# Attention and a gated MLP on one core: 29 of 36 weight tiles prepared beside the MLP's products, a second score tile turned by DMA, rows to combine loaded earlier

## The chip, the cores and the metric

The kernel runs on one core of a Trainium2 chip. The core has five engines that work side by side, each through its own queue of instructions in order: PE (TensorE, matrix products; PEld is its loading of weights), DVE (VectorE), ACT (ScalarE), POOL (GpSimd) and SP (SyncE, which here issues the DMAs). They meet through semaphores alone. The metric is the time of one execution in microseconds (us). Before the change it is 2955.62 us, the median of three runs (2955.44 to 2955.67).

## What is computed

The reference is one transformer block of 2048 rows and width 576: a normalisation modulated by a condition c, attention with 32 query heads over the last 512 keys of 16 cached heads, a residual, a second modulated normalisation, a gated MLP of width 4608, and a residual.

```python
mod = (silu(c) @ w_mod).reshape(1, 6, 1, -1)      # sa, ca, ga, sb, cb, gb
h = layernorm(x) * (1 + ca) + sa
q = (h @ wq) per head                             # 32 heads of 128
p = softmax(q @ k.T * 128 ** -0.5)                # 512 keys, head h uses cache head h // 2
x = x + ga * ((p @ v) @ wo)
h = layernorm(x) * (1 + cb) + sb
x = x + gb * ((silu(h @ w1) * (h @ w3)) @ w2)
```

All of it is done to about fp32's precision: each operand of a product is split into a high part (fp32r, as PE rounds it) and a low part, the rest, and three products stand for one.

## The kernel before

**Attention.** The 2048 rows are four blocks of 512. A *slot* is one head with one block, 128 of them (`slots`, numbers 0 to 127); slots 0 to 63 hold blocks 0 and 1, the others blocks 2 and 3. A slot has four *steps*, one for each tile of 128 rows. In a step PE makes the scores of a tile (L466 to L468), DVE their maximum (L470) and ACT the exponential (L479, `weights`). The tile p must then be turned, keys to the partitions, as two fp16 parts. That is done in one of two ways. By PE (`turn_by_pe`): three steps after the exponential four transposes against the identity (L505) put it into a PSUM bank of `t_bank` (two of them), ACT makes the high part (L509) and DVE the low one (L515). By DMA (`halve`, then `turned_by_dma`, L351): the exponential itself goes to a bank of `t_bank`, ACT and DVE make the two parts from there, and a transposing DMA, issued two steps after the low part, turns both. `BY_DMA` names the tiles of a slot that go by DMA: tile 0. At the end of the next slot PE multiplies with the values (L530, `values`) and over the following steps with the output weights into the bank pe (L428), which DVE adds into the rows `acc` (L547). Between these stand the query projections (`quad`, matrix qy and qx at L797): a product of two row blocks by two halves of weights is done with seven products instead of eight (Strassen's scheme, names p1 to p7), and so needs seven prepared combinations of the rows (`hdram`) and seven of each weight tile (`wdram`).

**Preparation beside attention.** ACT and POOL prepare these combinations ahead, in DRAM. `set_piece` does a weight tile: load 768 KB raw, four sums on POOL, for each of seven combinations a rounding on ACT (L692), two low parts on POOL (L697, L698), and a store. `rows_pieces` does the same for w2, `h_item` for the rows. `lay` spreads these items over the steps from number 13 on and again from 272 on: it gives each piece a POOL cost, keeps a pace (`PACE`), issues an item's loads (`fill`) `LEAD` = 3 steps before its first piece, and emits a piece's sums, high part, low part and store in four successive steps (`work`). There are 36 gate and up tiles (f = 0 to 35) and 19 pieces of w2, and the rows of three of four families.

**The MLP.** `mlp` runs 72 *groups* (m0 to m71): 36 tiles f with rows 0 to 1023 and then the same tiles with rows 1024 to 2047. A group is seven products p1, p2, p6, p7, p5, p3, p4 (L797, sums in the banks py and px) with one or two *down* products after most of them (`down`, L910), which alternate between the banks pe and pf. DVE adds each into `acc` or `sums` (L904), and only then can PE use that bank again. A group gives the gated activations of 128 columns for two row blocks; an even group and the odd one behind it make the pair that the down products of the next two groups use. After p2 DVE adds (L991), after p5 adds (L999), after p3 multiplies (L1003), after p4 adds and multiplies (L1005, L1006). `act_steps` makes the high and low parts of the activations: ACT L109, the low ones L110 on POOL (one of seven on DVE), and sums on POOL (L943, L950, L958, L959). The prepared set of the next group is loaded tile by tile (`load_wset`, L789) into a pool of eight buffers, tag w. During groups 12 to 30 POOL and ACT also combine rows 1024 to 2047 (`combine`, `stage`, L605 to L635). At groups 37 and 38 `finish` and `finish_rows` add up the first 1024 rows, on POOL and DVE. `split_x` subtracts one half of a block's columns from the other on POOL (L1220), for the second pair of blocks in group 14.

`acc`, the raw weights and the rows to combine share four wide buffers (tag x); in the MLP all four hold `acc`.

`at(slot or group, step, task)` puts a task behind a step; `run` emits what stands there. The order on each engine is the order in which the program emits it.

Of the kernel before, what the change touches and what calls it, by code (L numbers as in the profile page):

```python
# [8 lines left out]
F32 = mybir.dt.float32  # L9
F32R = mybir.dt.float32r  # L10
# [7 lines left out]
P = 128  # L18
# [16 lines left out]
EARLY, LATE = 13, 68  # L35
A1_AT, M0_AT = 24, 70
M0_ITEM = 16
ROOM, LEAD = 600, 3
WLEAD = 4
PACE = 3300, 3100  # L40
MORE, A1_ITEM = 0, 3

ORDERED = {mybir.EngineType.PE, mybir.EngineType.DVE, mybir.EngineType.Activation, mybir.EngineType.Pool, mybir.EngineType.SP}
SCALE = float(DH) ** -0.5
LIFT = 2.0**14
BY_DMA = (0,)
AFTER_EXP = 3
SETTLE = 2
TINY = 1e-30
# [3 lines left out]
def tile_block(  # L53
# [39 lines left out]
    def t_bank():  # L93
        return tpool.tile([P, 512], F32, tag="T", name="pt")
# [378 lines left out]
    def weights(i, t, pss, nm):  # L473
        st = state[i]
        turn(4 * i + t)
        if t == 0:
            st["l"] = odd.tile([P, ST], F32, tag="l", name="l", bufs=4)
        p = t_bank() if t in BY_DMA else pool.tile([P, SB], F32, tag="p", name="p", bufs=PB)
        nc.scalar.activation(p, pss, AF.Exp, bias=nm, accum_out=st["l"][:, t : t + 1])  # L479
        st["p", t] = p  # L480

    due, ways = {}, {}

    def into(st):
        if "pt" not in st:
# [3 lines left out]
    def halve(g):  # L489

        i, t = divmod(g - 1, 4)
        if 0 <= g - 1 < 4 * n and t in BY_DMA:
            st = state[i]
            p12 = pool.tile([P, 2, SB], F16, tag="p", name="p12", bufs=PB)
            nc.scalar.activation(p12[:, 0, :], st["p", t], AF.Copy, scale=LIFT)
            due.setdefault(g, []).append((st.pop(("p", t)), p12[:, 0, :], p12[:, 1, :], (t, p12)))

    def turn_by_pe(g):

        i, t = divmod(g - AFTER_EXP, 4)  # L500
        if 0 <= i < n and t not in BY_DMA:
            st = state[i]
            p, ps = st.pop(("p", t)), t_bank()
            for j in range(KC):
                nc.tensor.transpose(ps[:, j * P : (j + 1) * P], p[:, j * P : (j + 1) * P], ident)  # L505
            cols = slice(t * P, (t + 1) * P)
            ps = ps.rearrange("p (j n) -> p j n", j=KC)
            hi, lo = (into(st)[:, e, :, cols] for e in range(2))
            nc.scalar.activation(hi, ps, AF.Copy, scale=LIFT)  # L509
            due.setdefault(g, []).append((ps, hi, lo, None))  # L510
# [162 lines left out]
    def set_piece(f, n):  # L673

        def views():
            return [works[f][:, k] for k in range(6)]

        k, which = (("p2", 1), ("p1", 0), ("p4", 3), ("p5", 4), ("p6", 5), ("p7", 2), ("p3", 1))[n]

        def prep():  # L680
            a11, a12, a21, a22, s1, s2 = views()
            if n == 0:
                nc.gpsimd.tensor_add(s1, a21, a22)
                nc.gpsimd.tensor_sub(s2, s1, a11)
            elif n == 1:
                nc.gpsimd.tensor_sub(a21, a11, a21)
            elif n == 6:
                nc.gpsimd.tensor_sub(a12, a12, s2)

        def high():  # L690
            x, t = views()[which], staging([P, DC + 1, P], "wmade")
            nc.scalar.copy(t[:, :3, :], x)  # L692
            return x, t

        def low(xt):
            x, t = xt
            nc.gpsimd.tensor_sub(t[:, 3:, :], x[:, :2, :], t[:, :2, :].bitcast(F32))  # L697
            nc.gpsimd.tensor_sub(t[DR:, 2, :], x[DR:, 2, :], t[DR:, 2, :].bitcast(F32))  # L698
            if n == 6:
                del works[f]  # L700

        def put_out(xt):
            nc.sync.dma_start(wdram[f, k][:, :, :], xt[1].bitcast(F32))

        return (0 if n == 6 else None, (2040, 1020, 0, 0, 0, 0, 1020)[n], 1200), (prep, high, low, put_out)

    DOWN = (("p4", "p7"), ("p6",), ("p1", "p5"), ("p2", "p3"))
    G = NF // 2
# [449 lines left out]

    mlp_items = []
    for p in range(G + 1):  # L1160
        mlp_items += [w_item(f) for f in (2 * p, 2 * p + 1) if p < G]
        mlp_items.append(r_item(p))

    def lay(items, first, STEP):

        spare = []

        def cost(task, args):
            if task is put:
                return {split_in: 1580, split_out: 1440}.get(args[2], 0)  # L1170
            return {gate: 1440, last_q: 1300, lower_v: 1300, norm_rows: 330, make_h: 1300}.get(task, 0)

        def pass_fixed(upto):
            while clock[0] < upto:
                fixed = sum(cost(*job) for job in tasks.get(divmod(clock[0], 4), ()))
                clock[1] = max(clock[1], clock[0] * STEP) + fixed
                clock[0] += 1

        clock = [first - 4, 0]
        step, ends = first, []  # L1180
        for number, (fill, pieces) in enumerate(items):
            begin = ends[number - 2] + 1 if number > 1 else first - LEAD + number
            at(*divmod(begin, 4), fill)
            step, when = max(step, begin + LEAD), []
            for (behind, ahead, after), jobs in pieces:
                if behind is not None:
                    step = max(step, when[behind] + 2)
                pass_fixed(step + 1)
                while clock[1] + ahead + after > (step + 1) * STEP + ROOM:
                    step += 1  # L1190
                    pass_fixed(step + 1)
                clock[1] += ahead + after
                when.append(step)
                work(step, *jobs)
            ends.append(step + 2)
        return step
# [14 lines left out]
    for g in range(last_group):  # L1211
        for k, name in enumerate(ORDER):
            if groups[g][1] == groups[g + 1][1]:
                at(("m", g), k, keep_wset, g, name)
            else:
                at(("m", g), k, load_wset, g + 1, name)
    def split_x(pair):

        a = acc[2 * pair + 1]
        nc.gpsimd.tensor_sub(a[:, :, :HALF], a[:, :, :HALF], a[:, :, HALF:])  # L1220

    for d in range(2 * G):
# [6 lines left out]
            times = ((4, (g, 2)), (3, (g, 4)))  # L1229
        for q, (i, t) in times:  # L1230
            at(("m", i), t, load_oset, d, q)
    for pair, i in ((0, ("m", 0)), (1, ("m", 14))):
        at(i, 0, split_x, pair)
    at(("m", 2), -1, begin_sums, 0)
    at(("m", 2 * G + 2), 3, begin_sums, 1)

# [60 lines left out]
    for b in (2, 3):  # L1297
        for t in range(ST):
            at(("m", b), t, norm_stats, b, t)
        at(("m", 4), 1, norm_root, b)  # L1300
    for b, g in ((2, 6), (3, 9)):
        at(("m", g), 0, norm_scale, b)
        for t in range(ST):
            at(("m", g), t, norm_rows, b, t)
        for m in range(DC + 1):
            at(("m", g + 1 + m // 3), 2 * (m % 3), store_h, "M1", b, m, "AS"[m % 2], "raw")
    at(("m", 12), -1, begin_parts, "M1")
    for c in range(3):
        g = 12 + 6 * c
# [247 lines left out]
```

## Time and profile before

| | |
|---|---|
| median of three runs | 2955.62 us |
| the profiled execution | 2954.41 us |
| its span, first to last instruction | 2952.6 us |
| mean granted clock of PE | 0.998 |
| slots 64 to 119 | about 896 to 1628 us |
| the MLP's first 36 groups | about 1712 to 2340 us |

The page and the answers of the trace give times from the span's start. A row of instructions reads: line, engine, operation, what it writes and from what it reads, shape, count, then busy time in us and the mean of one in ns, and what ended the idle time before them. In the order of time a row is: start, length, engine, line, operation, and in brackets the idle time before it with its releaser. Matmuls are pipelined, so the time that one costs is read from the start of the next.

### The profile page before, as it was taken

What the parts mean: (1) busy time and instruction counts of PE and PEld (TensorE: products, weight loads), DVE (VectorE), ACT (ScalarE), POOL (GpSimd) and SP (SyncE); (2) the same over time, 40 slices, a digit from 0 to 9 for tenths busy, and PEclk for the clock granted to TensorE, in tenths of its full rate; (3) what the DMA queues carried; (4) which work ended last, traced back from release to release, by engine and by line L of the source; (5) the groups of instructions that cost most, each with busy time, mean ns of one, the idle gap of its engine ahead of it and who ended that gap; (6) DMA issues with size and microseconds to landing.
All of it is one profiled execution on the core that took longest, in us unless ns stands there. A gap on an engine that the chain in (4) does not pass through costs nothing.

```text
span 2952.6 us, 47355 instructions
## 1 busy us (share of the span) xinstructions
PE 2903.8 (98%) x16056; PEld 2384.8 (81%) x16056; DVE 2011.1 (68%) x3149; ACT 1560.9 (53%) x3251; POOL 1751.2 (59%) x1884
## 2 busy tenths in 40 slices
PE   7999999999999999999999999999999999999999
PEld 6777777777777777777777778888888888888887
DVE  7877787777777877777777766555555555555556
ACT  6667777777656776677677543333333222222322
POOL 3678888888712877777878223355564544334345
PEclk9999999999999999999999999999999999999999
DMA  6989999999885999989889946677766766666664
GB/s 216 280 266 347 277 345 311 298 289 299 260 277 179 326 301 295 296 284 283 273 278 299 300 154 202 218 233 251 251 226 202 286 231 199 205 198 193 202 201 143
DMA packets 441205, 751.27 MB, mean 254 GB/s; under 512 B 185730, under 2 KB 185730, under 8 KB 437380
## 3 DMA queue, kind: packets, MB, share of 16 engines
q1 hardware_dynamic: 440964, 748.25, 79.1%
q8 instruction: 128, 2.10, 0.3%
q14 instruction: 113, 0.93, 0.1%
HBM read 474.97 MB, written 235.37 MB: 241 GB/s over the span
## 4 chain that ended last, share of the span: by engine, by line
PE 80%; DVE 7%; ACT 4%; issue 2%; POOL 1%; DMA 1%; SPq 0%; ACTq 0%; POOLq 0%; DVEq 0%
PE py L797 15%; PE px L797 11%; PE po L530 10%; PE pe L428 10%; PE pf L910 7%; PE pe L910 7%; PE qy L797 5%; PE pt L505 4%; PE qx L797 3%; PE pss L466 2%; PE pss L468 2%; PE pss L467 2%; DVE nm L470 1%; DVE pt L515 1%; DVE acc L547 1%
## 5 line engine op out<-in xcount | busy, mean ns | idle before, releaser
L797 PE MATMUL py<-hset,wset 128*128 128x512 f32 x2016 | 507.2, 391 | 0.0
L547 DVE SCALAR_TENSOR_TENSOR acc<-pe,r,acc 128x576 f32<-128x576 f32 x510 | 413.6, 811 | 58.1 <-PE pe L428 55.4
L797 PEld LDWEIGHTS py<-hset,wset 128*128 128x128 f32 x2016 | 362.4, 188 | 59.0 <-ACT u L998 0.2
L428 PEld LDWEIGHTS pe<-o,oth 128*128 128x128 f32 x2040 | 319.7, 188 | 79.4 <-DVE acc L547 41.6
L797 PE MATMUL px<-hset,wset 128*128 128x512 f32 x1512 | 380.5, 391 | 0.0
L428 PE MATMUL pe<-o,oth 128*128 128x288 f32 x2040 | 360.1, 298 | 12.9 <-DVE acc L547 11.8
L530 PE MATMUL po<-pt,v 128*128 128x512 f16 x1536 | 353.8, 380 | 0.3 <-DMA v<-vs 0.3
L470 DVE TENSOR_REDUCE nm<-pss 128x1 f32<-128x512 f32 x512 | 345.6, 675 | 7.3 <-PE pss L468 7.1
L479 ACT ACTIVATE p<-pss,nm 128x512 f32<-128x512 f32 x384 | 265.7, 692 | 144.7 <-DVE nm L470 141.5
L697 POOL TENSOR_TENSOR wmade<-wraw,wmade 128x256 fp32r<-128x256 f32 x364 | 272.8, 749 | 115.5 <-issue 49.5
L110 POOL TENSOR_TENSOR akv<-u,akv 128x512 fp32r<-128x512 f32 x141 | 182.7, 1307 | 228.8 <-ACT akv L109 227.9
L797 PEld LDWEIGHTS px<-hset,wset 128*128 128x128 f32 x1512 | 275.5, 188 | 49.4
L509 ACT ACTIVATE pt<-pt 128x512 f16<-128x512 f32 x384 | 229.7, 598 | 136.6 <-PE pt L505 134.9
L535 DVE SCALAR_TENSOR_TENSOR otl<-po,undo,oth 128x512 fp32r<-128x512 f32 x128 | 96.1, 751 | 278.7 <-ACT oth L534 272.9
L515 DVE SCALAR_TENSOR_TENSOR pt<-pt 128x512 f16<-128x512 f32 x384 | 261.7, 681 | 28.7 <-ACT pt L509 28.3
L530 PEld LDWEIGHTS <-v 128*128 128x128 f16 x1536 | 140.6, 98 | 160.3 <-DMA v<-vs 0.6
L505 PEld LDWEIGHTS pt<-ident,p 128*128 128x128 f32 x1536 | 186.0, 140 | 72.0 <-PE pss L468 15.7
L505 PE MATMUL pt<-ident,p 128*128 128x128 f32 x1536 | 231.2, 273 | 9.4 <-DVE pt L515 6.4
L797 PE MATMUL qy<-hset,wset 128*128 128x512 f32 x784 | 237.0, 413 | 0.0
L466 PE MATMUL pss<-kh,qh 128*128 128x512 f32 x512 | 227.2, 444 | 6.3 <-ACT qh L109 2.2
L428 PE MATMUL pe<-o,otl 128*128 128x288 f32 x1020 | 217.5, 294 | 0.0
L468 PE MATMUL pss<-kh,ql 128*128 128x512 f32 x512 | 201.3, 393 | 0.9 <-DVE ql L110 0.9
(250 smaller groups left out, 5974.9 us busy)
## 6 DMA issues: line engine op xcount, KB each, us to landing
oset<-od SPq DMA_DIRECT2D x106, 576.0 KB, 4.7
od<-omade SPq DMA_DIRECT2D x133, 288.0 KB, 4.1
wraw<-in_B_w SPq DMA_DIRECT2D x36, 768.0 KB, 6.4
kept<-o SPq DMA_DIRECT2D x64, 288.0 KB, 5.1
o<-kept SPq DMA_DIRECT2D x32, 576.0 KB, 5.8
wraw<-in_A_wq_pairs SPq DMA_DIRECT2D x16, 768.0 KB, 6.3
w2raw<-in_B_w SPq DMA_DIRECT2D x38, 288.0 KB, 4.3
oset<-od SPq DMA_DIRECT2D x35, 288.0 KB, 3.2
```

The costliest lines, as they stand in the source:

```text
L428: nc.tensor.matmul(ps[:, h, :HALF], a[:, rows], b[:, h * HALF : (h + 1) * HALF], start=n == 0, stop=n == 2)
L466: nc.tensor.matmul(pss, st["qh"][:, rows], kh, start=True, stop=False)
L468: nc.tensor.matmul(pss, st["ql"][:, rows], kh, start=False, stop=True)
L470: nc.vector.tensor_reduce(nm, pss, axis=AX.X, op=ALU.max, negate=True)
L479: nc.scalar.activation(p, pss, AF.Exp, bias=nm, accum_out=st["l"][:, t : t + 1])
L505: nc.tensor.transpose(ps[:, j * P : (j + 1) * P], p[:, j * P : (j + 1) * P], ident)
L515: nc.vector.scalar_tensor_tensor(lo, p, LIFT, hi, op0=ALU.mult, op1=ALU.subtract)
L530: nc.tensor.matmul(po, v[:, d, j, :], pt[:, e, j, :], start=k == 0, stop=k == 3 * KC - 1)
L547: nc.vector.scalar_tensor_tensor(a, ps[:, :, :HALF], st["r"][:, t : t + 1], a, op0=ALU.mult, op1=ALU.add)
L697: nc.gpsimd.tensor_sub(t[:, 3:, :], x[:, :2, :], t[:, :2, :].bitcast(F32))
L797: nc.tensor.matmul(ps, w[:, a, :], h[:, b, :], start=start and n == 0, stop=n == 6, skip_group_check=True)
L910: nc.tensor.matmul(ps[:, h, :HALF], a[:, rows], w[:, b, :], start=m == 0, stop=m == 2)
```

## The change

- **Weight tiles.** `mlp_items` keeps only tiles f < `MADE_LATE` = 7. Tiles 7 to 35 are prepared in the group before the one that uses them: `load_raw` two groups ahead, then for each of the seven combinations `make_high` (the sums on POOL, the rounding on ACT, straight into the buffer that PE reads) behind the step at which `load_wset` stood, `make_low` (the two low parts, on DVE) one step later, and, for the tiles that the second pass loads, `keep_set` (the store) four steps later. The items that remain in `lay` move up: the last ends at step 351 (slot 87), before at step 486.
- **Spills.** Blocks 2 and 3 of `acc` are spilled in group 4 and loaded again in groups 34 and 35; the rows for their normalisation are loaded apart (`fetch_rows`), and `split_x` of the second pair moves from group 14 to group 37, behind step 5.
- **Tiles by DMA.** `BY_DMA` has three sets of tiles with the slots at which they begin and end: tile 0, and tiles 0 and 2 in slots 64 to 119 (65 to 120 counted from one).
- **Rows to combine.** Where an item is one of rows, its first piece comes `FAR` = 3 steps later behind its loads.

PE in slot 96, steps 0 to 1, from the scores (pss) through the transposes (pt), the projection (qy) and the output product (pe); before:

```order
L505 MATMUL pt<-ident,p 128x128 x4
L797 MATMUL qy<-hset,wset 128x512 x3
L428 MATMUL pe<-o,oth 128x288 x4
L428 MATMUL pe<-o,otl 128x288 x2
L466 MATMUL pss<-kh,qh 128x512
L467 MATMUL pss<-kl,qh 128x512
L468 MATMUL pss<-kh,ql 128x512
L505 MATMUL pt<-ident,p 128x128 x4
L797 MATMUL qy<-hset,wset 128x512 x4
```

The same place after (lines have moved):

```order
L510 MATMUL pt<-ident,p 128x128 x4
L828 MATMUL qy<-hset,wset 128x512 x3
L429 MATMUL pe<-o,oth 128x288 x4
L429 MATMUL pe<-o,otl 128x288 x2
L467 MATMUL pss<-kh,qh 128x512
L468 MATMUL pss<-kl,qh 128x512
L469 MATMUL pss<-kh,ql 128x512
L828 MATMUL qy<-hset,wset 128x512 x4
```

The four transposes of step 1 are gone; they turned tile 2 of the slot before.

DVE where group 33 passes to group 34, from p3's multiplication to the first down products of group 34 (u, s: activations; aal: a low part; acc: output rows); before:

```order
L1003 TENSOR_TENSOR u_27093<-u_27093,s_27123 128x512
L110 TENSOR_TENSOR aal<-u_27093,aah 128x512
L1005 TENSOR_TENSOR u_27052<-px,u_27052 128x512
L1006 TENSOR_TENSOR u_27052<-u_27052,s_27011 128x512
L904 TENSOR_TENSOR acc_21163<-pe,acc_21163 128x576
L904 TENSOR_TENSOR acc_21168<-pf,acc_21168 128x576
```

After, with the low parts of set 34 (wset from wraw, for p5, p3 and p4):

```order
L1034 TENSOR_TENSOR u_26494<-u_26494,s_26529 128x512
L111 TENSOR_TENSOR aal<-u_26494,aah 128x512
L730 TENSOR_TENSOR wset<-wraw,wset 128x256
L731 TENSOR_TENSOR wset<-wraw,wset 64x128
L1036 TENSOR_TENSOR u_26447<-px,u_26447 128x512
L1037 TENSOR_TENSOR u_26447<-u_26447,s_26399 128x512
L935 TENSOR_TENSOR acc_19806<-pe,acc_19806 128x576
L730 TENSOR_TENSOR wset<-wraw,wset 128x256
L731 TENSOR_TENSOR wset<-wraw,wset 64x128
L730 TENSOR_TENSOR wset<-wraw,wset 128x256
L731 TENSOR_TENSOR wset<-wraw,wset 64x128
L935 TENSOR_TENSOR acc_19811<-pf,acc_19811 128x576
```

One pair of low parts now stands between DVE's L110 and the addition that frees the bank pe, two more pairs before the one that frees pf.

POOL at the same place, sums and low parts of activations (u, aal, akv); before:

```order
L958 TENSOR_TENSOR u_26948<-u_26948,u_27093 128x512
L959 TENSOR_TENSOR u_26904<-u_26948,u_26904 128x512
L110 TENSOR_TENSOR aal<-u_26904,aah 128x512
L110 TENSOR_TENSOR akv<-u_26948,akv 128x512
```

After, with three of the four sums of set 35 (wraw; s1, s2 and the difference for p2):

```order
L989 TENSOR_TENSOR u_26322<-u_26322,u_26494 128x512
L990 TENSOR_TENSOR u_26272<-u_26322,u_26272 128x512
L716 TENSOR_TENSOR wraw<-wraw 128x384
L717 TENSOR_TENSOR wraw<-wraw 128x384
L111 TENSOR_TENSOR aal<-u_26272,aah 128x512
L719 TENSOR_TENSOR wraw<-wraw 128x384
L111 TENSOR_TENSOR akv<-u_26322,akv 128x512
```

The sums s1 and s2 follow the activations' sums directly.

The diff, cut to its core:

```diff
-ROOM, LEAD = 600, 3
+ROOM, LEAD, FAR = 600, 3, 3
+MADE_LATE = 7
-BY_DMA = (0,)
+BY_DMA = ((0,), (0, 2), (0, 2)), (64, 80, 120)
...
-        p = t_bank() if t in BY_DMA else pool.tile([P, SB], F32, tag="p", name="p", bufs=PB)
+        p = t_bank() if t in by_dma(i) else pool.tile([P, SB], F32, tag="p", name="p", bufs=PB)
...
+    def by_dma(i):
+        (few, more, most), (a, b, c) = BY_DMA
+        return few if i < a or i >= c else more if i < b else most
...
+    def make_high(f, k):
+
+        a11, a12, a21, a22, s1, s2 = [works[f][:, j] for j in range(6)]
+        if k == "p1":
+            nc.gpsimd.tensor_add(s1, a21, a22)
+            nc.gpsimd.tensor_sub(s2, s1, a11)
+        elif k == "p2":
+            nc.gpsimd.tensor_sub(a21, a11, a21)
+        elif k == "p7":
+            nc.gpsimd.tensor_sub(a12, a12, s2)
+        x = {"p1": a11, "p2": a12, "p6": s2, "p7": a21, "p5": s1, "p3": a12, "p4": a22}[k]
+        t = sets[f, k] = pool.tile([P, DC + 1, P], F32R, tag="w", name="wset", bufs=8)
+        nc.scalar.copy(t[:, :3, :], x)
+        works[f, k] = x, t
+
+    def make_low(f, k):
+
+        x, t = works[f, k]
+        nc.vector.tensor_sub(t[:, 3:, :], x[:, :2, :], t[:, :2, :].bitcast(F32))
+        nc.vector.tensor_sub(t[DR:, 2, :], x[DR:, 2, :], t[DR:, 2, :].bitcast(F32))
+        if k == ORDER[-1]:
+            del works[f]
+
+    def keep_set(f, k):
+        nc.sync.dma_start(wdram[f, k][:, :, :], works.pop((f, k))[1].bitcast(F32))
...
-        mlp_items += [w_item(f) for f in (2 * p, 2 * p + 1) if p < G]
+        mlp_items += [w_item(f) for f in (2 * p, 2 * p + 1) if f < MADE_LATE]
...
-            step, when = max(step, begin + LEAD), []
+            step, when = max(step, begin + LEAD + FAR * (fill.__name__ == "fill")), []
...
+            elif MADE_LATE <= g + 1 < NF:
+                for late, task in enumerate((make_high, make_low, keep_set)[: 2 + (g + 2 < NF)]):
+                    m, step = divmod(8 * g + k + 1 + late * late, 8)
+                    at(("m", m), step - 1, task, g + 1, name)
             else:
                 at(("m", g), k, load_wset, g + 1, name)
+    for f in range(MADE_LATE, NF):
+        at(("m", f - 2), 4, load_raw, f)
...
-    for pair, i in ((0, ("m", 0)), (1, ("m", 14))):
-        at(i, 0, split_x, pair)
+    for pair, i in ((0, ("m", 0)), (1, ("m", NF + 1))):
+        at(i, 5 * pair, split_x, pair)
...
+        at(("m", 4), 2, spill, b)
+        at(("m", NF + b - 2), (4, 0)[b - 2], load_x, b)
     for b, g in ((2, 6), (3, 9)):
+        at(("m", g - 1), 4, fetch_rows, b)
...
+        at(("m", g + 2), 3, rows.pop, b)
```

More of the change, by code (lines that the diff above doesn't have):

```diff
@@ L491, in halve @@
         i, t = divmod(g - 1, 4)
-        if 0 <= g - 1 < 4 * n and t in BY_DMA:
+        if 0 <= g - 1 < 4 * n and t in by_dma(i):
             st = state[i]
@@ L500, in turn_by_pe @@
         i, t = divmod(g - AFTER_EXP, 4)
-        if 0 <= i < n and t not in BY_DMA:
+        if 0 <= i < n and t not in by_dma(i):
             st = state[i]
```

## The prediction

> **What bounds the kernel now.** I read the page's busy shares first, then the busy time by stage, then who waited for whom on PE, and last the order of time at the places that the change touches.
>
> ```profile
> PE 2903.8 (98%) x16056; PEld 2384.8 (81%) x16056; DVE 2011.1 (68%) x3149; ACT 1560.9 (53%) x3251; POOL 1751.2 (59%) x1884
> ...
> 900.00:1628.00 728.00, 720.38 (x4065) 563.30 (x4065) 558.49 (x903) 510.21 (x1146) 542.77 (x695) 1.00 0.90 284
> 1712.00:2340.00 628.00, 627.04 (x3424) 550.70 (x3423) 356.77 (x506) 207.53 (x359) 294.67 (x228) 1.00 0.68 227
> ```
>
> The columns of the stages are length, then busy time of PE, PEld, DVE, ACT and POOL, granted clock, DMA share and GB/s. The first stage holds slots 64 to 119, where tiles are to be turned by DMA; the second is the gate and up products of the first 1024 rows, where the weights are now to be prepared. PE is busy for 720 of 728 and 627 of 628 us at full clock. So only two things can shorten this kernel, less work on PE or the few waits of PE in the attention slots; and any new wait of PE is lost in full. In the product stage DVE is busy for 57%, ACT for 33%, POOL for 47%.
>
> Who waited on PE between 896 and 1628 us (total, times, longest):
>
> ```profile
> PE pt L505 <- DVE pt L515: 2.7, 13, 0.3
> PE pe L428 <- DVE acc L547: 2.1, 4, 0.7
> PE pt L505 <- DVE p L515: 1.8, 1, 1.8
> ...
> PEld pe L428 <- DVE acc L547: 13.7, 31, 1.1
> ...
> PEld pt L505 <- DVE pt L515: 5.1, 25, 0.7
> ```
>
> No wait of PE ends in POOL, in a prepared weight or in a DMA. Taking weight preparations out of these slots therefore buys nothing by itself; it only makes room.
>
> **Part one: tiles turned by DMA.** 56 slots lose one group of four transposes. On PE such a group stands between the scores and the projection (start, length):
>
> ```profile
> 1307.63 0.60 PE L505 MATMUL pt<-ident,p 128*128 128x128 f32 x4
> 1307.98 0.94 PE L797 MATMUL qy<-hset,wset 128*128 128x512 f32 x3
> ```
>
> The next product starts 0.35 us later: 56 x 0.35 = 19.6 us off PE. ACT's and DVE's operations for the tile are the same by either way. In step 1 of a slot DVE used to take two lower halves (tiles 0 and 2), in step 3 none; now each step has one, and a PSUM bank of the turned tiles has two steps until it is used again. I take the PE waits for that (2.7 + 1.8) and a little of PEld's as gone, 5 us, and 3 of the accumulator's 15.8 (part of them follow DVE operations that POOL holds up, which the next part shows). Gain: 19.6 + 5 + 3 = 27.6 us. If DVE's pace takes half of the freed time back it is 10; if every wait above goes too it is 45.
>
> A sentence apart: the Trainium skill (VectorE: DVE Perf Modes, The three transpose paths and Rules for kernel authors) gives a 128x128 transpose 390 ns on TensorE and 1309 ns by DMA, and says to turn on TensorE where PSUM will do, against this part. By its 390 ns the 224 transposes would be 87 us instead of 19.6 (estimate), and the sum below 68 us lower, 2905; the row, 0.35 us for four, decides, and the advice to stay on TensorE does not fit a kernel in which PE is the engine that is short.
>
> **Part two: 29 weight sets prepared beside the products.** A set has seven tiles. ACT rounds each (seven casts a group), POOL makes four sums a set, and the low parts, on POOL before, are now 14 subtractions a set on DVE, from two operands in SBUF.
>
> ```profile
> L684 POOL TENSOR_TENSOR wraw<-wraw 128x384 f32<-128x384 f32 x26 | 26.9, 1035 | 2.0
> ...
> L692 ACT CAST wmade<-wraw x364: 495/510/557, 176.7 to 1610.7; 128x384 fp32r<-128x384 f32 x182
> ```
>
> The first products of two groups that lie two apart give a group's length:
>
> ```profile
> 2292.60 1.76 PE L797 MATMUL py<-hset,wset 128*128 128x512 f32 x7
> ...
> 2326.06 1.76 PE L797 MATMUL py<-hset,wset 128*128 128x512 f32 x7
> ```
>
> 33.46 / 2 = 16.7 us. ACT gets 7 x 0.51 = 3.6 us in it: hidden, it is busy for a third. POOL gets 4 x 1.03 = 4.1. For DVE's new operations there is no row; DVE takes 0.69 us for 512 and 0.74 for 576 elements (rows below), about 1 ns an element, so about 0.43 and 0.30 us for 256 and 128, 0.55 for both as they overlap. Unhindered that is 3.9 us a group, inside the 43% that DVE is idle. The DMA share of 0.68 has room for one 768 KB load a group more.
>
> What is not hidden shows in how DVE and POOL meet. From the attention slots, in order of time:
>
> ```profile
> 1342.04 1.00 POOL L683 TENSOR_TENSOR wraw<-wraw 128x384 f32<-128x384 f32 x1
> 1342.13 1.46 DVE L400 SCALAR_TENSOR_TENSOR kl<-kraw,kh 128x512 fp32r<-128x512 f32 x1
> 1343.12 1.32 POOL L684 TENSOR_TENSOR wraw<-wraw 128x384 f32<-128x384 f32 x1
> ```
>
> L400 reads two SBUF operands. It takes 1.46 us instead of 0.69 and ends 0.55 us after the POOL operation that was running, which is its own work; the POOL operation behind it is held up in turn, 1.32 instead of 1.0. And after one such DVE operation the waiting POOL operation comes first:
>
> ```profile
> 2359.93 1.30 POOL L858 TENSOR_TENSOR acc<-acc 128x288 f32<-128x288 f32 x1
> ...
> 2359.87 0.69 DVE L110 TENSOR_TENSOR aal<-u,aah 128x512 fp32r<-128x512 f32 x1 [0.69 <-ACT aah L109]
> 2360.48 1.36 DVE L867 TENSOR_TENSOR acc<-acc,sums 128x576 f32<-128x576 f32 x1
> ```
>
> L858 waits for L110, then L867 for L858, to 0.61 us past its end. So each of the 14 can meet a POOL operation of its own, and where POOL has a queue it does. Standing apart: the Trainium skill (SBUF — State Buffer, SBUF: two separate sides) says the same against this part, that whichever of a GpSimd operation and a VectorE operation with two SBUF inputs starts first keeps the shared ports for the whole instruction; the trace agrees, with the 0.55 us.
>
> Now **place A**, where an odd group passes to an even one (before, at group 33):
>
> ```profile
> 2292.49 1.23 DVE L110 TENSOR_TENSOR aal<-u,aah 128x512 fp32r<-128x512 f32 x1 [0.69 <-ACT aah L109]
> 2293.65 0.68 DVE L1005 TENSOR_TENSOR u<-px,u 128x512 f32<-128x512 f32 x1
> 2294.36 1.07 DVE L1006 TENSOR_TENSOR u<-u,s 128x512 f32<-128x512 f32 x1
> 2295.35 0.74 DVE L904 TENSOR_TENSOR acc<-pe,acc 128x576 f32<-128x576 f32 x1
> ...
> 2293.25 1.62 POOL L959 TENSOR_TENSOR u<-u,u 128x512 f32<-128x512 f32 x1
> ...
> 2296.59 0.42 PE L910 MATMUL pe<-oset,aah 128*128 128x288 f32 x2
> ```
>
> PE's down product at 2296.59 needs the bank pe, which L904 frees at 2296.09: half a us to spare. After the change the two low operations of p5 stand between L110 and L1005, and POOL has its sums s1 and s2 right behind L959. The first low waits for L959's end, 2294.87, and ends 0.29 later (0.43 less the 0.14 by which L400 was quicker, 0.55 for 0.69); s1 goes next, to 2296.1; the second low ends at 2296.25, L1005 at 2296.85, L1006 after s2 (2297.15) at 2297.7, L904 at 2298.4. PE waits 1.8 us. If both lows pass before s1, L904 ends at 2297.5: 0.9 us. If nothing got in their way, 0.05. The place comes 14 times: 14 x 1.8 = 25 us, at least 13.
>
> **Place B**, even to odd group:
>
> ```profile
> 2276.01 0.71 DVE L1006 TENSOR_TENSOR u<-u,s 128x512 f32<-128x512 f32 x1
> ...
> 2278.47 0.76 DVE L904 TENSOR_TENSOR sums<-pe,sums 128x576 f32<-128x576 f32 x1 [1.08 <-PE pe L910]
> ...
> 2276.80 1.29 POOL L950 TENSOR_TENSOR s<-u,u 128x512 f32<-128x512 f32 x1 [0.63 <-DVE u L1006]
> ...
> 2282.26 0.96 PE L910 MATMUL pe<-oset,akv 128*128 128x288 f32 x6
> ```
>
> With the lows of p5 ahead, L1006 ends about 2277.3, L950 at 2278.6; then the four lows of p3 and p4 alternate with L950, s1, s2 and the difference for p2 (1.03 each), to 2282.0, and L904 ends at 2282.7: PE waits 0.5 us, 14 x 0.5 = 7; nothing if the lows pass in pairs, 1.9 each (27) if DVE brings a delay of 1.4 from the group before.
>
> While the second half's rows are combined POOL has more to do:
>
> ```profile
> L608 POOL TENSOR_TENSOR hst<-hc,hst 128x512 fp32r<-128x512 f32 x14 | 19.1, 1363 | 18.3 <-ACT hst L605 18.3
> L613 POOL TENSOR_TENSOR hst<-hc,hst 32x512 fp32r<-32x512 f32 x14 | 18.7, 1335 | 8.9 <-issue 6.5 <-ACT hst L605 0.9 <-POOL u L943 0.8
> ...
> L1220 POOL TENSOR_TENSOR acc<-acc 128x1152 f32<-128x1152 f32 x1 | 2.7, 2693 | 0.0
> ```
>
> These 28 and 12 differences, 40 of 1.35 us, can each hold DVE for half their length, 27 us; PE waits at two places of the group only, so I take 10. The subtraction L1220 moves from group 14, where it was hidden, to group 37, where POOL has finish's rows queued and the first down product of the next group adds into the same rows: 3 us, at least 0. Loss: 25 + 7 + 10 + 3 = 45 us, between 13 and 82.
>
> **Part three** (rows to combine 3 steps ahead, spills, reloads) touches SP and DMA: nothing, as no wait of PE above ends there; 2 us either way.
>
> **The sum.** The profiled execution took 2954.4 us, 1.8 more than its span; the median is 2955.6. 2954.4 - 27.6 + 45 = 2971.8; 1.2 more for the median: 2973.
>
> **The rivals.**
> *DVE's lows find the ports free* (faster). If POOL's sums run early and both lows pass together, the loss is 13 to 20 us: 2955.6 - 27.6 + 13 to 20, about 2943. For it: POOL is busy for only 47%. Against: POOL's order at A puts four operations in a row. It decides where the loss of a pair of groups falls below 1.75 us (14 x 1.75 + 3 = 27.5). 0.25.
> *They cancel*, within 6 us of before (0.2%, about what a measurement here can tell from no change): 0.1.
> *DVE becomes the bound.* DVE's base is 0.57 x 16.7 = 9.5 us a group. With the 14 lows it has some 16 operations with two SBUF operands; if each waits 0.6 us, half of a POOL operation, it needs 9.5 + 3.9 + 9.6 = 23 us of 16.7. PE's waits would give POOL time to catch up, so I take the upper loss, 82, and not 29 x 6: about 3010. 0.1.
> *The turned tile comes late* (slower).
>
> ```profile
> 1299.61 1.31 SPq L351 DMA_TRANSPOSE pt<-p  x1
> ...
> 1317.42 0.39 PE L530 MATMUL po<-pt,v 128*128 128x512 f16 x1
> ...
> DMA to landing us min/median/max: 3.0/4.1/7.5
> ```
>
> Tile 0's transfer is issued 17.8 us before the values need it; tile 2's would be two steps (5.3 us) later, 12.5 us before, against 7.5 at worst, with a lighter SP queue. Only past 12.5 us to land would PE wait; at 14 in each slot it would be 56 x 1.5 = 84 us, about 3057. 0.03.
>
> **How the numbers follow.** The forecast case, the ports cost more than the transposes give, has 0.52, its own range 2962 to 3000. Faster by over 0.2%: 0.25 and a little of the forecast's low side, 0.28. Same 0.1; slower 0.62. The range 2934 to 3004 takes in the faster rival and leaves the last two and the ends out.
>
> **What would show it.** Right: slots 64 to 119 shorter by some 28 us in all; from group 7 to 34 the low subtractions on DVE at 0.7 to 1.5 us instead of 0.43, PE waiting on pe and pf for L904's successor, and groups of 18 to 19 us instead of 16.7. Wrong: DVE's lows near 0.43 us and groups at 16.7, which would leave the gain whole; transfers of turned tiles that land over 12 us after issue; PE waits on POOL in the attention slots that the trace of before does not have.

## The result and the profile after

The changed kernel takes 3045.4 us (median of four runs, 3044.9 to 3047.9) where the kernel before took 2955.6 beside it: ratio 1.0304, interval 1.0286 to 1.0322. It is slower, as forecast, by 90 us and not by 17, and outside the range. The span of the profiled execution is 3043.9 us, before 2952.6.

The page of the changed kernel, busy times and two rows of the forty slices:

```profile
PE 2914.0 (96%) x15832; PEld 2372.4 (78%) x15832; DVE 2293.6 (75%) x3555; ACT 1567.6 (52%) x3251; POOL 1516.7 (50%) x1478
...
PE   7999999999999999999999999988888999999999
...
DVE  7877787777778877777777669999999855555556
```

PE is busy a little longer though it has 224 instructions less, DVE 283 us longer, and PE reads 8 in five of the seven slices where DVE reads 9: the gate and up products of the first 1024 rows. By stage (slots 64 to 119, then groups 10 to 31):

```profile
900.00:1620.00 720.00, 710.44 (x3893) 550.86 (x3892) 559.24 (x910) 441.63 (x958) 190.75 (x199) 0.99 0.71 193
...
1880.00:2340.00 460.00, 400.03 (x2055) 338.98 (x2054) 436.27 (x597) 186.71 (x373) 303.81 (x243) 0.97 0.67 231
```

In the second stage DVE is busy for 436 of 460 us, PE for 400 where it was busy for all of the time, POOL for 304. The waits of PE between 1700 and 2400 us (before, between 1712 and 2330 us, there was one of 1.0 us):

```profile
PE pe L941 <- DVE sums L935: 27.0, 14, 2.6
PE pe L941 <- DVE acc L935: 20.1, 11, 2.7
PE pf L941 <- DVE sums L935: 11.1, 6, 2.9
PE pf L941 <- DVE acc L935: 9.0, 7, 2.5
```

These four end in the DVE addition that frees a bank of the down products (L935, L904 before). Of the 20.1 us for pf, 19.2 lie in groups 13 to 31, at the down product behind place A of the prediction and at the one ahead of place B. And what DVE newly does, over all 29 sets (min, median, max in ns):

```profile
L730 DVE TENSOR_TENSOR wset<-wraw,wset x203: 407/730/1553, 1817.4 to 2402.8; 128x256 fp32r<-128x256 f32 x102
L731 DVE TENSOR_TENSOR wset<-wraw,wset x203: 287/984/1429, 1817.8 to 2403.3; 64x128 fp32r<-64x128 f32 x102
```

The shortest are close to the estimate of the prediction (0.43 and 0.30 us). The medians are 0.73 and 0.98, and the smaller operation is the longer one.

Where the 91.3 us of the spans lie (group lengths from first product to first product, slots from the first product with the values to the next slot's): groups 6 to 35 of the MLP +97.2 in sum, from +0.5 to +7.3 each; group 38 +2.6; slots 64 to 119 -17.2 (732.3 to 715.1); slots 0 to 63 +7.5, of which 5.9 in slots 6 and 7; the rest 1. The second pass of the MLP behind group 38 is the same to 0.1 us.

Place A of the prediction at groups 33 to 34, in the order of time, DVE, POOL, then PE:

```profile
2380.04 1.51 DVE L730 TENSOR_TENSOR wset<-wraw,wset 128x256 fp32r<-128x256 f32 x1
2381.57 1.01 DVE L731 TENSOR_TENSOR wset<-wraw,wset 64x128 fp32r<-64x128 f32 x1
2382.61 0.69 DVE L1036 TENSOR_TENSOR u<-px,u 128x512 f32<-128x512 f32 x1
...
2379.65 1.62 POOL L990 TENSOR_TENSOR u<-u,u 128x512 f32<-128x512 f32 x1
2381.23 1.20 POOL L716 TENSOR_TENSOR wraw<-wraw 128x384 f32<-128x384 f32 x1
...
2384.78 0.53 PE L941 MATMUL pe<-oset,aah 128*128 128x288 f32 x2 [1.63 <-DVE acc L935]
```

It went as worked out: the first low ends 0.28 us behind L990 (L959 before), POOL's s1 comes next, the second low ends 0.15 behind that, and PE waits 1.63 us (forecast 1.8). Place B at groups 32 to 33:

```profile
2359.52 1.54 DVE L730 TENSOR_TENSOR wset<-wraw,wset 128x256 fp32r<-128x256 f32 x1
...
2362.12 0.69 DVE L1037 TENSOR_TENSOR u<-u,s 128x512 f32<-128x512 f32 x1
2362.73 0.75 DVE L935 TENSOR_TENSOR sums<-pf,sums 128x576 f32<-128x576 f32 x1
2363.40 1.07 DVE L730 TENSOR_TENSOR wset<-wraw,wset 128x256 fp32r<-128x256 f32 x1
2364.48 1.01 DVE L731 TENSOR_TENSOR wset<-wraw,wset 64x128 fp32r<-64x128 f32 x1
2365.52 1.19 DVE L730 TENSOR_TENSOR wset<-wraw,wset 128x256 fp32r<-128x256 f32 x1
2366.72 0.99 DVE L731 TENSOR_TENSOR wset<-wraw,wset 64x128 fp32r<-64x128 f32 x1
2367.74 0.76 DVE L935 TENSOR_TENSOR sums<-pe,sums 128x576 f32<-128x576 f32 x1
...
2359.50 1.28 POOL L111 TENSOR_TENSOR akv<-u,akv 128x512 fp32r<-128x512 f32 x1 [1.20 <-issue]
2362.89 1.29 POOL L981 TENSOR_TENSOR s<-u,u 128x512 f32<-128x512 f32 x1 [2.11 <-DVE u L1037]
...
2359.63 1.76 PE L828 MATMUL py<-hset,wset 128*128 128x512 f32 x7
...
2368.56 1.05 PE L941 MATMUL pe<-oset,akv 128*128 128x288 f32 x6 [2.36 <-DVE sums L935]
```

Four lows in a row take 4.26 us instead of 1.4, each one POOL operation, and PE waits 2.36 us where the forecast had 0.5: the low of p5 ahead met POOL's L111 (1.54 us), so that L1037 ends 3.2 us behind the group's first product (2359.63), where L1006 ended 0.8 us behind it.

### The profile page after: what moved, and what is told of

It reads as the page before. It is cut to its first block, busy times and chain, and to the rows that moved or that the text cites. A ratio compares the mean times of both kernels' runs of the same rounds, so it can differ in the third digit from the quotient of the medians.

```text
span 3043.9 us, 46569 instructions
## 1 busy us (share of the span) xinstructions
PE 2914.0 (96%) x15832; PEld 2372.4 (78%) x15832; DVE 2293.6 (75%) x3555; ACT 1567.6 (52%) x3251; POOL 1516.7 (50%) x1478
## 4 chain that ended last, share of the span: by engine, by line
PE 66%; DVE 15%; issue 5%; ACT 4%; DMA 3%; POOL 2%; SPq 1%; DVEq 0%; ACTq 0%; POOLq 0%
PE py L828 11%; PE pe L429 10%; PE po L535 10%; PE px L828 8%; PE pe L941 5%; PE pf L941 5%; PE qy L828 4%; PE qx L828 3%; PE pt L510 3%; PE pss L467 2%; PE pss L468 2%; PE pss L469 2%; DVE wset L731 2%; DVE wset L730 2%; DVE nm L471 1%
## 5 line engine op out<-in xcount | busy, mean ns | idle before, releaser
L828 PE MATMUL px<-hset,wset 128*128 128x512 f32 x1512 | 389.0, 397 | 2.9 <-DVE u L1030 1.6
L429 PE MATMUL pe<-o,oth 128*128 128x288 f32 x2040 | 362.6, 300 | 17.7 <-DVE acc L552 15.5
L480 ACT ACTIVATE p<-pss,nm 128x512 f32<-128x512 f32 x328 | 226.1, 689 | 157.5 <-DVE nm L471 152.3
L118 POOL TENSOR_TENSOR ql<-qv,qh 128x512 fp32r<-128x512 f32 x28 | 36.1, 1290 | 534.5 <-ACT qh L117 483.9
L514 ACT ACTIVATE pt<-pt 128x512 f16<-128x512 f32 x328 | 196.0, 597 | 148.8 <-PE pt L510 148.0
L111 POOL TENSOR_TENSOR akv<-u,akv 128x512 fp32r<-128x512 f32 x141 | 186.6, 1333 | 170.9 <-ACT akv L110 159.9
L520 DVE SCALAR_TENSOR_TENSOR pt<-pt 128x512 f16<-128x512 f32 x328 | 223.8, 682 | 34.4 <-ACT pt L514 34.1
L1023 ACT ACTIVATE s<-s 128x512 f32<-128x512 f32 x72 | 45.6, 633 | 307.9 <-DVE s L1022 307.9
L510 PEld LDWEIGHTS pt<-ident,p 128*128 128x128 f32 x1312 | 160.6, 140 | 54.7 <-PE pss L469 8.4
```

Source lines behind the costliest of these rows:

```text
L429: nc.tensor.matmul(ps[:, h, :HALF], a[:, rows], b[:, h * HALF : (h + 1) * HALF], start=n == 0, stop=n == 2)
L520: nc.vector.scalar_tensor_tensor(lo, p, LIFT, hi, op0=ALU.mult, op1=ALU.subtract)
L828: nc.tensor.matmul(ps, w[:, a, :], h[:, b, :], start=start and n == 0, stop=n == 6, skip_group_check=True)
```

## The experiments

**Theory:** a low on DVE waits for whatever POOL has running, lets POOL's next one in, and the next low waits for that; so DVE becomes the bound of the groups. **Rivals:** 14 more operations are too many for DVE by their plain length; the combining of rows, the rounding on ACT or POOL's sums do it by themselves; or the parts of the change disturb one another. The first three runs take the change apart.

```diff
 # before, tiles alone
-BY_DMA = (0,)
+BY_DMA = ((0,), (0, 2), (0, 2)), (64, 80, 120)
```

> The tile part alone: in slots 64 to 119 two of four tiles are turned by DMA, the weights are prepared in the attention slots as before, rows to combine are loaded as before. Theory (the whole loss of the change lies in the products of the first 1024 rows): those groups stay at 16.7 us and slots 64 to 119 become 10 to 20 us shorter, 2936 to 2946 us. Rival (the transposes need the room that the weights left: the DMA engines were busy for 0.90 of these slots before): turned tiles land late, PE waits on DMA in the values, 2955 us or more.

2948.0 us, ratio 0.9973 (0.9964 to 0.9983): faster, a little less than expected. Groups stay at 16.7 us, slots 64 to 119 take 723.1 us, 9.2 less than before and 8 more than in the changed kernel. The rival has a part of it:

```profile
900.00:1620.00 720.00, 706.16 (x3848) 545.76 (x3847) 561.00 (x903) 509.20 (x1148) 541.14 (x695) 0.99 1.03 308
...
PE po L534 <- DMA pt<-p: 4.4, 2, 2.2
```

With the weights still prepared in these slots the DMA engines are full (share 1.03), and in slots 72 to 93 (298 us, before 292) single slots take up to 18 us; in the other 34 the gain is whole, 14.8 us. Two of PE's long waits in those slots (2.1 and 2.2 us, slots 73 and 93) are for a turned tile; the longest, 3.5 us in slot 89, is for ACT, which itself waits 4.7 us for a store of combined rows to land (hdM0p<-hst).

```diff
 # changed kernel, weights and loads alone
-BY_DMA = ((0,), (0, 2), (0, 2)), (64, 80, 120)
+BY_DMA = ((0,), (0,), (0,)), (64, 80, 120)
```

> The changed kernel with one tile of four turned by DMA in all slots, so with the weights and the loads moved alone. Theory: the groups of the first 1024 rows are as long as in the changed kernel (about 97 us more than before in sum), slots 64 to 119 lose their gain of 17 us or most of it: 3052 to 3065 us. Rival (the turned tiles and the prepared weights cost each other something): 3045 us or less.

3065.8 us, ratio 1.0371 (1.0356 to 1.0386), at the upper end of what the theory has: groups +100.4, slots 64 to 119 at 732.1 us, as before. Moving the weights out of these slots bought nothing by itself. Tiles alone give -8.6, weights alone +109; together +90. The room that the weights leave is worth some 10 us to the tiles.

```diff
-ROOM, LEAD, FAR = 600, 3, 3
+ROOM, LEAD, FAR = 600, 3, 0
```

> The changed kernel with the rows to combine loaded as early as before (FAR 0 instead of 3). Theory (the shift by three steps is what lengthens slots 6 and 7 by 6 us, and what puts the rows of the third and fourth hundred beside the late turned tiles of slots 74 to 85): slots 0 to 63 as before, 847 us instead of 855, in all 3030 to 3040 us. Rival (it is the prepared weights' absence or the DMA load in slots 74 to 85, and slots 6 and 7 are chance): 3043 to 3047 us.

3036.5 us, ratio 1.0273 (1.0256 to 1.0290): 9 us less than the changed kernel, and slots 0 to 63 take 846.6 us, as before (847.4). Theory right there. With FAR = 3 POOL waits in slots 6 and 7 on a DMA on which it did not wait before (between 100 and 260 us, changed kernel):

```profile
POOL hst L1167 <- DMA hdA0p<-hst: 7.9, 2, 6.6
```

That this wait is the link is read from the trace alone. In slots 74 to 85 little changed (slot 76 takes 16.1 us, in the changed kernel 17.3, before 14.9): that half of the theory falls.

Now the lows. Each of the next five starts from the changed kernel. They and the two behind them were timed once each; their group lengths are from the trace of that execution.

```diff
-        nc.vector.tensor_sub(t[:, 3:, :], x[:, :2, :], t[:, :2, :].bitcast(F32))
-        nc.vector.tensor_sub(t[DR:, 2, :], x[DR:, 2, :], t[DR:, 2, :].bitcast(F32))
+        nc.scalar.copy(t[:, 3:, :], x[:, :2, :])
+        nc.scalar.copy(t[DR:, 2, :], x[DR:, 2, :])
```

> The changed kernel with the low tiles written by ACT as copies of the first input: the subtraction is left out, DVE gets no new operation at all, POOL's sums and ACT's rounding stay. Theory (DVE's low operations are the whole loss of the groups): groups of 16.7 to 17.2 us, 2945 to 2962 us. Rival (POOL's sums, by holding the operations that DVE had before, or the rounding on ACT, make a part of it): over 2975 us.

2949.6 us, groups +1.8 in all. So DVE's lows are the whole loss of the groups; POOL's sums, the combining and ACT's rounding cost PE nothing without them, although ACT has 14 copies more here.

```diff
 # as the run above, and
+        nc.vector.tensor_reduce(r[:, :1], x[:, :2, :].rearrange("p a n -> p (a n)"), axis=AX.X, op=ALU.max)
+        nc.vector.tensor_reduce(r[DR:, 1:], x[DR:, 2, :], axis=AX.X, op=ALU.max)
```

> As the run with copies on ACT, and DVE takes the maximum of each row of the same inputs at the places of the 14 low operations (128x256 and 64x128, one SBUF operand, a column of results), so that it has as many operations of about the plain length of the lows (estimate 0.35 and 0.2 us by 0.68 for 512 elements). Theory (it is the waiting for POOL and not the plain load of 14 operations): they take their plain length beside POOL's operations, and the time is within 12 us of the run with copies on ACT. Rival (plain load, or DVE waits for POOL with any SBUF operand): 40 us or more above it.

2962.1 us, 12.5 above the run with copies, half a us more than the theory allows and far from the rival's 40. The operations on DVE:

```profile
L733 DVE TENSOR_REDUCE u<-wraw x203: 401/409/422, 1813.4 to 2318.0; 128x1 f32<-128x256 f32 x102
L734 DVE TENSOR_REDUCE u<-wraw x203: 282/282/285, 1813.8 to 2318.4; 64x1 f32<-64x128 f32 x102
```

They are as long as unhindered lows (0.41 and 0.29), stand at the same places beside the same POOL operations, and not one of 406 is lengthened. Groups +17.7: the plain length of 14 operations is 16 of the 97 us at most, the rest comes with the waiting. The reductions do not read ACT's rounded tile, as the lows do, but that is not the difference: in the changed kernel DVE was never idle ahead of L730 or L731.

```diff
-        nc.vector.tensor_sub(t[:, 3:, :], x[:, :2, :], t[:, :2, :].bitcast(F32))
+        nc.vector.tensor_scalar(t[:, 3:, :], x[:, :2, :], 1.0, None, op0=ALU.mult)
 # and likewise the smaller
```

> The changed kernel in which each of the 14 low operations a set multiplies its first input by one on DVE instead of subtracting the rounded tile: as many operations of the same sizes at the same places, but the subtraction is left out, and each reads one SBUF operand. Theory (a DVE operation with two SBUF operands waits for the POOL operation in progress): they take 0.41 and 0.29 us or less instead of 0.78 and 0.72, groups fall from 21 to 17 or 17.5 us, 2945 to 2965 us. Rival (14 more operations ahead of the accumulations in DVE's order are too many by themselves): groups stay over 19 us, 3000 us or more.

3011.8 us, groups +65.4: my expectation failed.

```profile
L730 DVE TENSOR_SCALAR wset<-wraw x203: 275/534/1442, 1815.3 to 2367.4; 128x256 fp32r<-128x256 f32 x102
L731 DVE TENSOR_SCALAR wset<-wraw x203: 224/226/1293, 1815.6 to 2367.7; 64x128 fp32r<-64x128 f32 x102
```

With one SBUF operand this operation waits too, up to 1.44 us, though its own length is 0.28, less than for two operands. So the number of operands was the wrong mark; the reduction, which also reads one, is free. The Trainium skill (SBUF — State Buffer, SBUF: two separate sides) has VectorE take the shared ports for two SBUF inputs and also in a 2-port performance mode; the 0.28 us beside 0.41 and the waits agree with it.

```diff
 # make_high: POOL's four sums a set left out
-        if k == "p1":
-            nc.gpsimd.tensor_add(s1, a21, a22)
...
```

> The changed kernel without POOL's four sums for each set that is prepared beside the products (left out: the prepared tiles are then those of other halves). DVE's 14 low operations a group keep both operands. Theory (the lows wait for whatever POOL has running, and the sums are about half of that): lows fall to 0.5 to 0.6 us in the mean, half of the 97 us of the groups goes, 2985 to 3005 us. Rival (the sums hardly matter, POOL's other operations or DVE's own load do): 3030 us or more.

2996.3 us, groups +48.6: half, as the theory has it, though the means of the lows fell less than it says. The larger low's median is now 0.425 us, the smaller's 0.290 (means 0.65 and 0.59: POOL's other operations remain).

```diff
 # combine and stage of rows 1024 to 2047: POOL's 40 operations left out
-            nc.gpsimd.tensor_sub(lo, x, hi.bitcast(F32))
+            nc.scalar.copy(lo, x)
...
-        sub = nc.gpsimd.tensor_sub
+        sub = lambda *a: None
```

> The changed kernel without POOL's 40 operations that combine the rows of the second half in groups 12 to 30 (their low parts are copied on ACT, their differences left out); the lows and POOL's sums stay. Theory (they lengthen POOL's queue, and with it what a low waits): groups 13 to 31 fall from 4.1 us over 16.7 in the mean to the 1.9 of groups 6 to 12, 41 us less, 3000 to 3012 us. Rival (they are POOL's affair alone): 3035 us or more.

3018.1 us, between the two expectations. Groups 13 to 31 fall from +77.0 to +48.8, still 2.6 each and not 1.9; the quiet ones (6 to 12, 32 to 35) are at +23.2. So the combining is worth 28 us in its groups. The waits of PE in this run between 1880 and 2360 us (pf: one in group 9):

```profile
PE pe L937 <- DVE sums L931: 27.0, 12, 2.4
PE pe L937 <- DVE acc L931: 21.4, 13, 1.8
PE pf L937 <- DVE acc L931: 0.9, 1, 0.9
```

The 19.2 us of waits for pf in groups 13 to 31 are gone. What stays is 1.6 us at place A and, in each odd group from 13 on, 2.3 to 2.4 us at place B, where groups 7, 9 and 11 wait about 1.0: the 1.9 us that I took from groups 6 to 12 was too small a measure. A second thing lengthened these groups. The trace of the changed kernel shows it, behind a wait of PE:

```profile
2216.89 1.76 PE L828 MATMUL py<-hset,wset 128*128 128x512 f32 x7
2221.12 0.85 PE L941 MATMUL pf<-oset,aah 128*128 128x288 f32 x2 [2.46 <-DVE acc L935]
...
2222.72 2.43 PE L828 MATMUL px<-hset,wset 128*128 128x512 f32 x7
...
2221.12:2224.30 3.18, 3.18 (x11) 2.85 (x12) 3.14 (x6) 2.61 (x6) 1.47 (x3) 0.53 0.90 339
```

Behind a wait of 2.46 us PE's granted clock is 0.53 for 3.2 us. The clock records of the trace have eight such stretches between 1720 and 2450 us, all in groups 14 to 31: the clock is 0.50 for 3.41 us, once for 6.83. Seven begin near the end of a wait of 2.1 to 2.9 us, the eighth behind one of 1.9, and their products stand 13.0 us further apart in sum than the same products elsewhere. Not every such wait does it: of the 15 of 2.1 us or more in groups 6 to 35, eight (2.3 to 2.7 us) left the clock full. In the run without combining there are six stretches, 9.7 us, and three of them in groups 13 to 31, 4.7 us. The Trainium skill (TensorE: Matmul & The Clock Gate, Part 1: The HAM clock gate) has the clock halved after an idle window of about 3.4 us; here it was halved behind waits of 1.9 to 2.9 us.

The last two put the lows elsewhere.

```diff
-        nc.vector.tensor_sub(t[:, 3:, :], ...)
-        nc.vector.tensor_sub(t[DR:, 2, :], ...)
+        nc.gpsimd.tensor_sub(t[:, 3:, :], ...)
+        nc.gpsimd.tensor_sub(t[DR:, 2, :], ...)
```

> The changed kernel with the 14 low operations a group on POOL, where they were in the attention slots (0.76 and 0.46 us there), not on DVE. By rows of before POOL then has 8.5 (its own of 16.7) + 4.1 (sums) + 8.5 (lows) = 21 us of work a group, 24 while the rows of the second half are combined. Theory (the engine that is short of room sets the group, whichever it is): groups of 20 to 24 us, 3050 to 3120 us. Rival (POOL's results are needed late, so its queue only slips): 3020 us or less.

3114.8 us, groups +166, as the theory has it. Between 1900 and 2300 us:

```profile
1900.00:2300.00 400.00, 334.79 (x1596) 284.56 (x1595) 162.52 (x216) 149.00 (x291) 377.54 (x430) 0.88 0.60 209
...
2103.36 1.76 PE L828 MATMUL py<-hset,wset 128*128 128x512 f32 x7
...
2110.08 3.35 PE L828 MATMUL py<-hset,wset 128*128 128x512 f32 x7 [3.39 <-ACT u L1029]
```

POOL is busy for 378 of 400 us, DVE for 163, and PE's clock is 0.88 over the stage: behind a wait of 3.39 us seven products take 3.35 us instead of 1.76. There are 23 such stretches between 1840 and 2460 us, and they cost some 54 us, counted as above.

```diff
-        nc.vector.tensor_sub(t[DR:, 2, :], x[DR:, 2, :], t[DR:, 2, :].bitcast(F32))
+        nc.gpsimd.tensor_sub(t[DR:, 2, :], x[DR:, 2, :], t[DR:, 2, :].bitcast(F32))
```

> The changed kernel with the 7 smaller low operations a group (64x128) on POOL and the 7 larger on DVE. Theory (each DVE operation that meets POOL's queue waits for one POOL operation, whatever its own length, so 7 wait where 14 did): about half of the waiting goes, 3000 to 3020 us. Rival (POOL's longer queue takes it back): 3035 us or more.

2993.2 us, groups +46.9: half, and below the range that I gave. In the quiet groups 16 of the 20.1 us go, where rows are combined 34 of the 77.0. Seven operations of DVE fewer, each plainly 0.29 us, free 50 us, where the plain length of all 14 was worth 16 at most; POOL takes 3.6 us more a group (median 0.52 each). It is still slower than before.

In us over before, by groups:

| run | groups 6 to 35 | 6 to 12, 32 to 35 | 13 to 31 | time |
|---|---|---|---|---|
| changed kernel | 97.2 | 20.1 | 77.0 | 3045.4 |
| one operand | 65.4 | 13.8 | 51.7 | 3011.8 |
| no sums on POOL | 48.6 | 9.4 | 39.3 | 2996.3 |
| small lows on POOL | 46.9 | 4.1 | 42.8 | 2993.2 |
| no combining on POOL | 72.1 | 23.2 | 48.8 | 3018.1 |
| copies on ACT, reductions on DVE | 17.7 | 5.9 | 11.9 | 2962.1 |
| copies on ACT | 1.8 | 0.0 | 1.8 | 2949.6 |
| all lows on POOL | 166.3 | 36.7 | 129.7 | 3114.8 |

**A kernel that beats both.** The tiles alone gain; the next slots were chosen by where the run with the tiles alone lost time.

```diff
 # before, and tiles 0 and 2 by DMA in
+        return BY_DMA[64 <= i < 72 or 94 <= i < 120]
```

> The kernel before with the second tile turned by DMA in slots 64 to 71 and 94 to 119 only, 34 slots, leaving out those in which the run with the tile part alone lost time to late tiles. Theory (a slot without a late tile is 0.38 us shorter): 34 x 0.38 = 13 us less than before, 2941 to 2946 us, some 5 us below the run with all 56 slots. Rival (the DMA engines are full in all of these slots, and the late tiles go elsewhere): 2948 us or more.

2939.8 us, ratio 0.9942 (0.9928 to 0.9955), 1.2 us below the range. Slots 64 to 119 take 718.9 us, 13.4 less than before, the 13 of the theory.

```diff
+        return BY_DMA[50 <= i < 72 or 94 <= i < 120]
```

> As the run with 34 slots, and the second tile is turned by DMA in slots 50 to 63 too, 48 slots. Theory: 14 x 0.38 = 5 us less than with 34 slots, 2936 to 2941 us. Rival (those slots are set by DVE, or turned tiles land late there): as with 34 slots or more.

2934.4 us, ratio 0.9928 (0.9915 to 0.9940), the fastest, and 1.6 us below the range. Slots 50 to 63 take 175.4 us, before 181.9. From slot 50 on and in the groups:

```profile
690.00:1620.00 930.00, 922.07 (x5109) 716.34 (x5108) 725.81 (x1178) 653.51 (x1459) 652.10 (x828) 1.00 0.99 299
1712.00:2340.00 628.00, 627.06 (x3421) 551.92 (x3420) 355.27 (x501) 201.27 (x350) 309.87 (x245) 1.00 0.69 231
```

The groups are as before. The DMA share is 0.99 from slot 50 on; whether still more slots would gain was not run.

## Why the prediction was wrong

- *Where the kernel is bound, and that no wait in the attention slots ends in a weight.* Right: with the weights alone moved, slots 64 to 119 keep their 732 us.
- *Gain of the tiles, 27.6.* Right in 34 slots: 64 to 71 and 94 to 119 are 16.2 us shorter, 0.48 each, and 27.6 / 56 is 0.49; where PE had no wait in a slot before, it is 0.38 in the mean, near the 0.35 for the transposes. In slots 72 to 93 the gain is 0.9 us instead of 11. The waits of PE and PEld between 900 and 1620 us:

```profile
PE pe L429 <- DVE acc L552: 4.1, 2, 3.9
PE po L535 <- ACT hf L581: 2.7, 1, 2.7
...
PEld pe L429 <- DVE acc L552: 12.5, 29, 4.3
```

  PE no longer waits for pt, as forecast, but as long for acc as before (there PEld 13.7), once for 3.9 us, and 2.7 us for the rows that ACT normalises in these slots. These two waits are most of what is missing in slots 76 and 84, which are 2.4 and 4.1 us longer than before. Behind both stands ACT, and ACT waits for a store of rows to land (start, length, and in brackets its idle time):

```profile
1072.33 0.78 ACT L581 ACTIVATE hf<-ps_n,shift_b,gain_b 128x512 f32<-128x512 f32 x1 [4.37 <-DMA hM<-hf]
...
1178.92 0.62 ACT L1162 CAST hst<-hc 128x512 fp32r<-128x512 f32 x1 [5.02 <-DMA hdM0p<-hst]
```

  The prediction asked whether the turned tiles would land late; it did not ask this of the other transfers.
- *Place A, 14 x 1.8 = 25.* Right: 1.63 us in the rows above, and the six even quiet groups are 2.0 us longer in the mean.
- *Place B, 14 x 0.5 = 7.* The step that failed by most, and it failed in its start: L1006 was taken to end 0.6 us later in its group than before; it ended 2.4 us later, as the low of p5 ahead of it met POOL's L111. From there on the lows and POOL's sums alternate as forecast. In the run without combining PE waits 2.3 to 2.4 us at B in every odd group from 13 to 33, and in sum the 15 odd groups are 41.5 us longer than before, some 6 of it by the lower clock. The upper end, 1.9 each with a delay of 1.4 us brought along, was nearer.
- *Combining, 10.* 28 us in groups 13 to 31 go with POOL's 40 operations. The step that failed is "PE waits at two places of the group only": with the combining PE waits at two more, 19.2 us for pf, and at neither without it. The other 8 are the lower clock behind longer waits (13.0 us in these groups, 4.7 without combining), for which the prediction had no term. Groups 13 to 31 are 42 us longer than the quiet ones would be (77.0 - 19 x 1.83); the 14 beyond the 28 are those 4.7 and about 9 from the longer waits at place B. DVE was idle for 24 of 460 us, so it had little time in which a delay could be made good; that this is why delays reach the product next to A and B is argued from that share.
- *split_x, 3.* Right: group 38 is 2.6 us longer.
- *Part three, nothing.* Wrong: FAR costs 9 us. It was judged by the waits of slots 64 to 119, though the first rows to combine stand in slots 2 to 9.
- *The sum.* -27.6 + 45 + 0 = +17 was forecast; -17.2 (slots 64 to 119) + 97.2 (groups) + 2.6 (group 38) + 7.5 (slots 0 to 63) + 1.2 (the rest) is the +91.3 of the spans.
- *The rivals.* DVE as the bound was the case that came, with chance 0.1. Its own working gave 23 us a group (groups 13 to 31 take 20.8) and was then cut to 82 us, since "PE's waits would give POOL time to catch up". POOL was idle for a third of the stage, and it did not help, as its operations come in rows right where DVE's do, as at A and B above. L730 and L731 together take 1.49 us in the mean against 0.70 plain: 7 x 0.8 = 5.6 us of waiting a group, of the 9.6 that this rival allowed for 16 operations. That lows find the ports free was refuted: 225 of the 406 take over 1.2 times the shortest. A late turned tile was no cost in the changed kernel (one PE wait of 0.3 us).

What stays open: why those stores of rows land late in slots 72 to 93, and why some waits of 2.3 to 2.7 us are followed by the lower clock and others not.

## What to carry to other kernels

Price a VectorE operation that waits for GpSimd by what GpSimd has running, and not by its own size (here a 64x128 subtraction of 0.29 us had a median of 0.98): count the operations, put few large ones, and look for where both queues are full. Where an engine with such waits is busy for nearly all of a stage (95% for DVE here), a sum over the places that the trace of before shows falls short: here PE came to wait at two more. Work that an off-path engine hides well in one stage (POOL beside attention) can be on the path in the next.

## What had not been expected of the hardware

- PE's granted clock falls to 0.50 for 3.4 us or more around the end of waits of 1.9 us and more, seven times of 15 from 2.1 us up: 13.0 us of the 97, and some 54 in the run with all lows on POOL. In the changed kernel one such wait cost 2.3 us more than itself.
- A multiplication by a constant from SBUF to SBUF on DVE waits for POOL like a subtraction of two tiles (0.22 to 1.29 us for 64x128), a row maximum of the same tile never does (0.282 to 0.285).
